# All expert weights of a fused attention and mixture-of-experts kernel pass through ten fixed staging places

## The chip, the cores and the metric

The kernel runs on 1 core of a Trainium2 chip. The metric is the device time of one execution in microseconds (us). The engines are TensorE (PE, matmuls; PEld is its weight load), VectorE (DVE), ScalarE (ACT), GpSimd (POOL) and SyncE (SP, which here only issues DMAs and register loads). Each engine works through its own list of instructions strictly in the order in which it is written, so an instruction that waits also holds whatever stands behind it.

## The reference, cut to what matters

```python
scores = scale * np.matmul(q, k.transpose(0, 1, 3, 2))       # 8 batches, 8 heads, 576 x 64
thresh = np.max(scores, axis=-1, keepdims=True) - tau
scores = np.where(scores >= thresh, scores, -1000000000.0)
attn = softmax(scores)
x = (attn @ v) as 4608 tokens x 512
logits = x @ w_gate ; expert_idx = argmax(logits)            # 8 experts, one for each token
for e in range(8):
    h = np.maximum(x[mask_e] @ w1[e], 0.0)                   # 512 -> 1024
    out[mask_e] = gate_w * (h @ w2[e])                       # 1024 -> 512
```

## The kernel before, in words

**Attention.** The 64 heads are taken in 32 pairs, n = 0 to 31, each in 11 steps (NSTEP), so the attention ends with step 352 (KEND). In a step PE forms a tile of scores of a later pair (s_unit, for the row maxima), a tile of transposed scores of the present pair (st_unit), and parts of the product with v (av_piece). Every operand is split into a high and a low 16-bit part. The operand tiles of four pairs rotate: QK (high and low parts of q and k), ck and CQ (low parts, constants and the rows of maxima), each refilled by DMAs on SP's queue (stack, parts). vf holds v of one group.

**Routing of a batch.** When the last head of a batch has left PSUM (evac), finish scales the tokens: row sums `rs` (L519, L520, L524, L525), tokens `xn` (L534), and their 16-bit parts into the rows `R` (L541 on ACT, L542 on DVE for the last batch). Each tile of 128 tokens is transposed by a DMA on SP's queue into `xTg` (L549); logits multiplies it by w_gate on PE (`lg`, L567, 12 small matmuls for each tile), route finds the expert on DVE (L597 to L608), and ranks counts on PE (`rk`, L616 to L619) where each token goes. send scatters the rows to a table in DRAM (L639), tables2 and tables3 work out which rows each block of an expert gathers, and fetch gathers them (L863) and transposes them (`xTm` or `spare`, L873).

**Experts.** Blocks of 128 tokens: four for each of experts 0 and 1, one at a time (g = 0 to 7), later ones in pairs. The first two blocks of expert 1 and all of expert 0 hold tokens that were placed before the last batch was routed, so their matmuls stand between the steps of that routing on PE. gemm1 makes `h` (L927, 96 matmuls of 128x128 for a block of 128), relu splits it into `hl` (L915 on ACT, L916 on DVE), gemm2 makes `y` (L960, 24 matmuls of 512 columns), leave scales it into `o` (L971).

**Weights.** An expert has 8 pieces of 512 KB (w = 0, 1 for w1 and w2, c = 0 to 3), listed in wseq. load_w reads a piece as 32-bit numbers into a staging tile, split_w makes its high part on ACT (L822) and its low part on DVE (L830; for expert 0 with a helping matmul, L256 and L257) into `wb1` or `wb2` of set e % 2. Expert 0's pieces pass through two tiles of the pool mp0 and, for its last two, through ck and CQ. The pool mp1, on the space that the attention's tiles leave (close), holds eight staging tiles for all later pieces; expert 1's eight loads are issued there from ACT's queue, everything later from SP's, each when the piece eight places earlier has been split (weights).

The order of each engine's list is set by a scheduler from the planned steps, so small moves in the plan can reorder instructions of all engines near the end of the attention.

Of the kernel before, what the change touches and what calls it, by code (L numbers as in the profile page):

```python
# [9 lines left out]
F16 = mybir.dt.float16  # L10
F32 = mybir.dt.float32
# [6 lines left out]
P = 128  # L18
B, H, S, D = 8, 8, 576, 64
DM, E, F = 512, 8, 1024  # L20
NTOK = B * S
NPAIR = B * H // 2
# [22 lines left out]
TUNE = dict(  # L45
    lead=10, cast=2, sl=8, ll=15, sp0=3, sps=0, lv=-16, sv0=-6, sv1=2, av=2, g=4, l=3, d=4, g5=4, l5=3, d5=2, g6=1, l6=2, d6=2, g7=1, l7=1, d7=1, off=2, off5=1, off6=5, lg=4, lg7=22, km=12, rate=40, dh=1, do=3, ws0=6, wsd=2, w1d=4, plv=1, xv=5, so=0, sto=0, ord=0, sc=6, fa=3, fd=4, wa1=-70, wa2=-86, wl1=-28, wl2=-6, avb=1, route=1, ranks=7, pp=8, ew=4, maskat=0, w1a=-38, w1b=4,
)
# [3 lines left out]
def kernel(  # L51
# [9 lines left out]
    nc = tc.nc  # L61
# [13 lines left out]
    apool = ExitStack()  # L75
    ldp = ExitStack()
    ld = ldp.enter_context(tc.tile_pool(name="ld", bufs=2, side="right"))
    xp = ctx.enter_context(tc.tile_pool(name="xp", bufs=2))
    op = apool.enter_context(tc.tile_pool(name="op", bufs=4))
    pp = apool.enter_context(tc.tile_pool(name="pp", bufs=8))  # L80


# [23 lines left out]
    NB = 2  # L106
    NQ = 4
    ck2 = [cpool.tile([P, 2, 2, S], F16, name=f"ck_{i}") for i in range(NQ // 2)]
    cq2 = [op.tile([P, 2, 9 * P], F16, tag=f"CQ{i}", name=f"CQ_{i}", bufs=1) for i in range(NQ // 2)]
    cks = [[ck2[i // 2][:, i % 2, a] for a in range(2)] for i in range(NQ)]  # L110
    cqs = [cq2[i // 2][:, i % 2] for i in range(NQ)]
    none = before[96:96 + NM, 0:64]
# [53 lines left out]
    gr = {}  # L166
# [10 lines left out]
    def plan(k, f, where=END):  # L177
        if urgent[0]:
            f = hurry(f)
        assert (k, where) >= (now[0], slot[0])  # L180
        acts.setdefault(k, ([], [], []))[where].append(f)
# [11 lines left out]
    def after(k, f, where=END):  # L193
        plan(now[0] + k, f, where)
# [27 lines left out]
        st[n] = dict(qkf=qkf, Ph={}, Pl={})  # L222

    def load_v(g):
        vf = op.tile([P, 2, 10, D], F32, tag="vf", name=f"vf_{g}", bufs=1)
        load = (nc.sync if g == 0 else nc.scalar).dma_start(vf, v[g])
        if g == 0:
            tc.keep_in_program_order(load)
        gr[g] = dict(vf=vf)

    def split(n, lag=1):

# [26 lines left out]
    def stack(n):  # L259
        d = st[n]  # L260
        hi, lo = d["hi"], d["lo"]
        d["CK"] = cks[n % NQ]
        d["QA"], d["KB"] = [], []

        d["CQ"] = CQ = cqs[n % NQ]
        if n >= NQ:
            nc.sync.dma_start(
                CQ[64:KC].rearrange("p (t c) -> p t c", t=18), none.unsqueeze(1).to_broadcast([NM, 18, 64])
            )
        for a in range(2):  # L270
            r = slice(64 * a, 64 * a + 64)
            QK = op.tile([P, 2, S], F16, tag=f"QK{a}", name=f"QK_{n}_{a}")
            nc.sync.dma_start(QK[0:64], hi[r])
            nc.sync.dma_start(QK[64:128, 0], lo[r, 0])
            nc.sync.dma_start(QK[64:128, 1], hi[r, 1])
            nc.sync.dma_start(d["CK"][a][0:64], lo[r, 1])
            d["QA"].append(QK[:, 0])
            d["KB"].append(QK[:, 1])
        for a in range(2):
            r = slice(64 * a, 64 * a + 64)  # L280
            nc.sync.dma_start(CQ[0:64, a * NT * P:(a + 1) * NT * P], hi[r, 0, 0:NT * P])
            nc.sync.dma_start(CQ[0:64, 8 * P + 64 * a:8 * P + 64 * a + 64], hi[r, 0, NT * P:S])

    def split_v(g, u):
        d = gr[g]
        vf = d["vf"]
        d["vop"] = vop = vops[g % NB]
        tc.keep_in_program_order(nc.scalar.activation(vop[:, u, :, 0:D], vf[:, u], AF.Copy, scale=SV))
        for i in range(2):
            t = slice(5 * i, 5 * i + 5)  # L290
            after(1, lambda i=i, t=t: low_part(
                vf[:, u, t], vop[:, u, t, 0:D], vop[:, u, t, D + 1:2 * D + 1], SV, f"v{g}_{u}_{i}"
            ), END if i else MID)
# [477 lines left out]
    NS = NEARLY + NL  # L771
    EARLY_SLOTS = sum(EARLY[1])
    wb1, wb2, pools = [], [], []
    slots = {}
    placed = {}

# [7 lines left out]
    wq = {}  # L784
    T = {}

    def open_pool(i):

        mp = ctx.enter_context(
            tc.tile_pool(name=f"mp{i}", bufs=2, side=("right", "left")[i], reuse_waits="tile")  # L790
        )
        pools.append(mp)
        wb1.append(mp.tile([P, 4, 2 * F], F16, name=f"wb1_{i}", bufs=1))
        wb2.append(mp.tile([P, 4, 2 * F], F16, name=f"wb2_{i}", bufs=1))

    def load_w(e, w, c):

        i = int(e != 0)
        if (e, w) == (0, 1) and c >= 2:
            wf = (ck2, cq2)[c - 2][0]  # L800
            wf = wf.rearrange("p a b s -> p (a b s)") if c == 2 else wf.rearrange("p a s -> p (a s)")
            wq[e, w, c] = wf = wf.bitcast(F32)[:, 0:F]
            nc.sync.dma_start(wf, w12[e, :, c, w])
            return
        wq[e, w, c] = wf = pools[i].tile([P, F], F32, tag="wf", name=f"wf_{e}_{c}_{w}", bufs=2 + 6 * i)
        if e in range(E):
            load = (nc.scalar if e == 1 else nc.sync).dma_start(wf, w12[e, :, c, w])
            if e == 1:
                tc.keep_in_program_order(load)
            return  # L810
        if e not in regs:
            regs[e] = nc.sync.value_load(T["esi"][0:1, e - E:e - E + 1], min_val=0, max_val=E - 1)
        nc.sync.dma_start(wf, w12[ds(regs[e], 1), :, c, w].rearrange("o p f -> (o p) f"))
# [185 lines left out]
    NSTEP = len(st_order)  # L999
# [4 lines left out]
    KEND = NSTEP * NPAIR  # L1004
    KM = KEND - TUNE["km"]
    NF = 3
    WS0, WSD = TUNE["ws0"], TUNE["wsd"]
    W1D = TUNE["w1d"]
    DH, DO = TUNE["dh"], TUNE["do"]
    PLV = {(NPAIR - 1, t) for t in ((), (1, REST), (1,), (REST,), (1, REST, 5), (1, 3, REST, 5, 7))[TUNE["plv"]]}  # L1010
    XV = {(B - 1, j) for j in range(TUNE["xv"])}
# [84 lines left out]
    def close():  # L1096
        apool.close()
        open_pool(1)
        for i, x in enumerate(wseq[8:16]):
            after(W1D * i, lambda x=x: load_w(*x))  # L1100

    wseq = [(0, w, c) for w in range(2) for c in range(4)]
    k = NSTEP * (NPAIR - 2) - LEAD - SL
    plan(k + 1, room)
    for i in range(8):
        t = k + WS0 + WSD * i if i < 4 else KEND + 1 + 2 * (i - 4)
        plan(t, lambda i=i: split_w(*wseq[i]))
        if i < 4:
            plan(t, lambda i=i: load_w(*wseq[i + 2]))
        elif i >= 6:  # L1110
            plan(NSTEP * (NPAIR - 2) + i - 4, lambda i=i: load_w(*wseq[i]))
    TABLES = {B - 3: tables0, B - 2: tables1, B - 1: tables2}
    plan(KEND + 12, close)

# [56 lines left out]
        last = -1 if e2 < 0 else NE * e2 + NE - 1 if e2 < E else NEARLY + e2 - E  # L1171
        return wseq[turn[0]] == (e, w, c) and (e, w, c) in wq and past[w] >= last

    asked = [8]

    def weights(j):
        turn[0] = j + 1
        split_done.add(wseq[j])
        split_w(*wseq[j])
        if j + 8 < len(wseq):  # L1180
            k, e = when[j][:2]
            moe(
                max(chunk[0] + 1, k - (14 if e == 2 else 24)) if e < E else chunk[0] + 1,
                lambda: asked[0] == j, lambda: (asked.__setitem__(0, j + 1), load_w(*wseq[j + 8])),
            )

    for j, (k, *x) in enumerate(when):
        moe(k, lambda x=x: may(*x), lambda j=j: weights(j + 8))

# [131 lines left out]
```

## Time and profile before

| what | value |
|---|---|
| time, median of 3 runs | 1016.65 us (1015.65 to 1017.06) |
| profiled execution, its own time | 1016.57 us |
| its span, first to last instruction | 1014.8 us |
| PE busy, share of the span | 949.3 us, 94% |
| DVE, ACT, POOL busy | 699.2, 653.9, 558.2 us |
| mean granted clock of PE, of full speed | 0.979 |

The profile divides the span into busy time of each engine; idle time in front of an instruction is put down to what it waited for last. The time of an execution holds 1.8 us around the span.

### The profile page before, as it was taken

The page shows a single profiled execution, that of the slowest core. Times are in us where ns is not written, and L with a number is a line of the kernel's source. Part 1 is how long each engine was busy: PE and PEld are TensorE (multiplying, and loading weights), DVE is VectorE, ACT ScalarE, POOL GpSimd, SP SyncE. Part 2 cuts the span into 40 slices and gives each one's busy share as a digit, 9 for nine tenths or more (in the row PEclk, how much of TensorE's full clock was granted, in tenths as well). Part 3 has the DMA queues.
Part 4 walks back from the last instruction along what each step waited for, and adds up shares of the span by engine and source line. Part 5 has one row for each costly group of instructions (what it writes and reads, how often), then busy time and mean ns, then how long its engine had stood idle before and what let it go on. Part 6 is the DMA issues. An engine that isn't in the chain of part 4 may idle for free. (4 is left out here: it accounts for less than half of the span.)

```text
span 1014.8 us, 28646 instructions
## 1 busy us (share of the span) xinstructions
PE 949.3 (94%) x11548; PEld 610.5 (60%) x11548; DVE 699.2 (69%) x1413; ACT 653.9 (64%) x1114; POOL 558.2 (55%) x470
## 2 busy tenths in 40 slices
PE   7799999999999999999998995979999999999997
PEld 2355555556565565565565863657766676667684
DVE  7899999988999898999996853715342433424560
ACT  2689897988988888989898843314342433424551
POOL 6466885996987969969879820341212222222121
PEclk9899999999999999999998998889999999999999
DMA  7553554563746645636458299788565755557730
GB/s 199 145 135 76 138 140 126 131 166 104 184 102 176 135 122 151 176 109 166 101 156 209 66 217 249 262 166 223 176 166 162 226 143 182 151 163 219 224 106 26
DMA packets 142749, 159.19 MB, mean 157 GB/s; under 512 B 96403, under 2 KB 112789, under 8 KB 142614
## 3 DMA queue, kind: packets, MB, share of 16 engines
q1 hardware_dynamic: 125446, 96.13, 38.2%
q10 hardware_dynamic: 7920, 31.74, 10.8%
q0 software_dynamic: 9248, 29.45, 8.9%
q8 instruction: 92, 1.51, 0.7%
q14 instruction: 43, 0.35, 0.1%
HBM read 90.24 MB, written 19.44 MB: 108 GB/s over the span
## 5 line engine op out<-in xcount | busy, mean ns | idle before, releaser
L436 POOL TENSOR_TENSOR pl<-e,ph 128x1024 f16<-128x1024 f32 x158 | 336.0, 2135 | 101.4 <-ACT ph L435 62.4
L427 ACT ACTIVATE e<-st,ntau 128x512 f32<-128x512 f32 (+1 forms) x352 | 222.8, 650 | 49.3 <-PE st L411 45.8
L430 DVE SCALAR_TENSOR_TENSOR e<-st,e 128x512 f32<-128x512 f32 (+1 forms) x352 | 219.8, 636 | 13.1 <-ACT e L427 12.5
L927 PEld LDWEIGHTS <-wb 128*128 128x128 f16 x2304 | 191.5, 99 | 31.5 <-issue 13.0
L927 PE MATMUL h<-xTm,wb 128*128 128x256 f16 (+2 forms) x2112 | 200.3, 254 | 8.7 <-issue 8.6
L960 PE MATMUL y<-wb,hl 128*128 128x512 f16 (+1 forms) x1056 | 205.2, 364 | 0.8 <-issue 0.8
L370 DVE TENSOR_REDUCE nm<-s 128x1 f32<-128x512 f32 x300 | 188.2, 633 | 19.1 <-PE s L360 17.0
L480 PE MATMUL av<-vop,ph 128*128 128x65 f16 (+3 forms) x3072 | 188.6, 195 | 3.0 <-ACT x L490 2.0
L480 PEld LDWEIGHTS <-ph 128*128 128x128 f16 (+1 forms) x3072 | 159.7, 100 | 48.3 <-issue 23.3
L480 PE MATMUL av<-vop,pl 128*128 128x65 f16 (+1 forms) x1536 | 168.3, 195 | 5.1 <-POOL pl L436 5.0
L435 ACT CAST ph<-e 128x1024 f16<-128x1024 f32 x160 | 166.4, 1040 | 6.6 <-DVE e L430 6.1
L480 PEld LDWEIGHTS <-pl 128*128 128x128 f16 (+1 forms) x1536 | 137.4, 100 | 36.4 <-issue 10.7
L960 PEld LDWEIGHTS <-hl 128*128 128x128 f16 (+1 forms) x1056 | 94.8, 101 | 101.2 <-issue 7.1
L830 DVE SCALAR_TENSOR_TENSOR wb<-wf,wb 128x1024 f16<-128x1024 f32 x88 | 104.0, 1221 | 68.2 <-ACT wb L822 65.6
L410 PE MATMUL st<-QK 128*128 128x512 f16 (+3 forms) x640 | 138.3, 293 | 3.3 <-DVE nm L370 0.9
L411 PE MATMUL st<-CQ,ck 128*128 128x512 f16 (+3 forms) x640 | 137.2, 288 | 2.3 <-issue 1.6
L974 POOL DMA_INDIRECT out_dram<-o,gt x40 | 43.4, 1085 | 167.5 <-ACT o L971 149.3
L358 PE MATMUL s<-QK 128*128 128x512 f16 (+1 forms) x600 | 129.1, 292 | 3.6 <-DVE e L430 2.7
L360 PE MATMUL s<-ck,CQ 128*128 128x512 f16 (+1 forms) x600 | 127.4, 287 | 1.5 <-DMA CQ<-hi 1.5
L915 ACT ACTIVATE hl<-h 128x512 f16<-128x512 f32 (+1 forms) x80 | 45.9, 573 | 120.5 <-PE h L927 97.9
L822 ACT ACTIVATE wb<-wf 128x1024 f16<-128x1024 f32 x94 | 95.9, 1051 | 37.1 <-DMA wf<-in_w_dram 19.3
L971 ACT ACTIVATE o<-y,gt 128x512 f32<-128x512 f32 (+1 forms) x40 | 26.6, 664 | 101.0 <-PE y L960 80.0
(199 smaller groups left out, 995.5 us busy)
## 6 DMA issues: line engine op xcount, KB each, us to landing
wf<-in_w_dram SPq DMA_DIRECT2D x86, 512.0 KB
qkf<-in_qk_dram ACTq DMA_DIRECT2D x30, 576.0 KB
vf<-in_v_dram ACTq DMA_DIRECT2D x15, 640.0 KB
QK<-hi SPq DMA_DIRECT2D x64, 144.0 KB
QK<-lo SPq DMA_DIRECT2D x64, 72.0 KB
QK<-hi SPq DMA_DIRECT2D x64, 72.0 KB
ck<-lo SPq DMA_DIRECT2D x64, 72.0 KB
CQ<-hi SPq DMA_DIRECT2D x64, 64.0 KB
```

Of the source, the lines that this page charges most:

```text
L358: nc.tensor.matmul(sc[rows, oc], d["QA"][a][:, cols], d["KB"][a][:, CH[c]], start=True, stop=False)
L360: nc.tensor.matmul(sc[rows, oc], d["CQ"][:, at:at + cols.stop - cols.start], d["CK"][a][:, CH[c]], start=False, stop=True,)
L370: nc.vector.tensor_reduce(o, sc[:, 0:width(t)], axis=AX.X, op=ALU.max, negate=True)
L410: nc.tensor.matmul(sc[rows, oc], d["KB"][a][:, cols], d["QA"][a][:, CH[c]], start=True, stop=False)
L411: nc.tensor.matmul(sc[rows, oc], d["CK"][a][:, cols], d["CQ"][:, q], start=False, stop=True)
L427: nc.scalar.activation(pf, sc, AF.Exp, bias=ntau, scale=0.125 / SS)
L430: nc.vector.scalar_tensor_tensor(pf, sc, 0.0, pf, ALU.is_ge, ALU.mult)
L435: nc.scalar.copy(h, pd)
L436: (nc.vector if (n, t) in PLV else nc.gpsimd).tensor_tensor(l, pd, h, ALU.subtract)
L480: nc.tensor.matmul(av[:, 0:D] if z == 2 else av, l if z == 1 else h, vop[:, tv, W:W + D] if z == 2 else vop[:, tv, 0:W], start=i in (0, NT ...
L927: nc.tensor.matmul(o, Wt[:, c, wh, f], x, start=c == 0 and z == 0, stop=c == 3 and z == 2,)
L960: nc.tensor.matmul(o, h[:, hh], Wt[:, f, wh, c], start=f == 0 and z == 0, stop=f == 7 and z == 2)
```

## The change

All weight pieces of all experts pass through ten fixed places (`stages`): the tiles of ck, CQ and QK of the attention, vf, and the two tiles of mp0. The attention's tiles become permanent (op moves to the outer pool, and QK is one tile of two halves for each of four pairs), and mp1 has no staging tiles any more. Expert 1's eight loads move from ACT's queue to SP's and are planned at steps 340 to 362 (the end of the attention is step 352); two pieces of expert 2 follow at once. A later piece j + 10 is asked for when piece j has been split, where it was j + 8. Expert 0's first splits move by up to four steps. Only load_w, the plan and the allocation change: what is multiplied and split stays the same.

```diff
-    op = apool.enter_context(tc.tile_pool(name="op", bufs=4))
+    op = ctx.enter_context(tc.tile_pool(name="op", bufs=1))
...
+    qks = [op.tile([P, 2, 2, S], F16, name=f"QK_{i}") for i in range(NQ)]
+    vf = op.tile([P, 2, 10, D], F32, name="vf")
...
+        if i == 0:
+            first_wf.extend(mp.tile([P, F], F32, name=f"wf_{z}", bufs=1) for z in range(2))
+            stages.extend([words(ck2[0], "a b s"), words(cq2[0], "a s"), words(qks[0], "a w s"), words(qks[1], "a w s")])
+            stages.append(vf.rearrange("p u t d -> p (u t d)")[:, 0:F])
+            stages.extend([words(qks[2], "a w s"), words(qks[3], "a w s"), words(cq2[1], "a s"), *first_wf])
...
-        wq[e, w, c] = wf = pools[i].tile([P, F], F32, tag="wf", name=f"wf_{e}_{c}_{w}", bufs=2 + 6 * i)
+        j = 6 + 4 * w + c if e == "x" else wseq.index((e, w, c))
+        wq[e, w, c] = wf = first_wf[j % 2] if j < 6 else stages[(j - 6) % len(stages)]
         if e in range(E):
-            load = (nc.scalar if e == 1 else nc.sync).dma_start(wf, w12[e, :, c, w])
+            load = nc.sync.dma_start(wf, w12[e, :, c, w])
...
         open_pool(1)
-        for i, x in enumerate(wseq[8:16]):
-            after(W1D * i, lambda x=x: load_w(*x))
...
-        t = k + WS0 + WSD * i if i < 4 else KEND + 1 + 2 * (i - 4)
+        t = k + (5, 7, 14, 16)[i] if i < 4 else KEND + 1 + 2 * (i - 4)
...
-            plan(t, lambda i=i: load_w(*wseq[i + 2]))
-        elif i >= 6:
-            plan(NSTEP * (NPAIR - 2) + i - 4, lambda i=i: load_w(*wseq[i]))
+            plan(t + 3, lambda i=i: load_w(*wseq[i + 2]))
+    for i, t in enumerate((336, 338, 340, 342, 344, 346, 356, 358, 360, 362)):
+        plan(t, lambda i=i: load_w(*wseq[6 + i]))
...
+    def ask(j):
+        if j < len(wseq):
+            k, e = when[j - 8][:2]
             moe(
-                max(chunk[0] + 1, k - (14 if e == 2 else 24)) if e < E else chunk[0] + 1,
-                lambda: asked[0] == j, lambda: (asked.__setitem__(0, j + 1), load_w(*wseq[j + 8])),
+                max(chunk[0] + 1, k - (16 if e == 2 else 24)) if e < E else chunk[0] + 1,
+                lambda: asked[0] == j, lambda: (asked.__setitem__(0, j + 1), load_w(*wseq[j])),
             )
```

**ACT, where the attention's last product has left PSUM.** Before, the row sums of the last batch (L519, L524) follow that evacuation at once, and ACT issues expert 1's first two loads (L807) itself:

```order
909 L490 COPY x_12084<-av_1_13212 128x4x65
910 L495 COPY xh_10427<-av_1_13212 64x65 x2
911 L519 ACTIVATE rs_13369<-x_12084 128x32
912 L524 ACTIVATE rs_13369<-xh_10427 128x8
913 L807 DMA wf_0_0_13393<-in_w_dram 128x1024
914 L915 ACTIVATE hl_0_13258<-h_1_13261 128x512
915 L541 CAST R<-xn_0_13410 128x4x128
916 L541 CAST R<-xn_1_13424 128x4x128
917 L807 DMA wf_1_0_13463<-in_w_dram 128x1024
918 L822 ACTIVATE wb_1_13390<-wf_0_0_13393 128x1024
```

The same place in the changed kernel, right after L490, L495 and two splits into wb_1 like the first row (its line 825 is line 822 of before, 918 is 915; vf, QK, CQ and wf are the staging places of expert 1's pieces):

```order
914 L825 ACTIVATE wb_1_13318<-vf 128x1024
915 L825 ACTIVATE wb_1_13318<-QK_121 128x1024
916 L825 ACTIVATE wb_1_13319<-QK_122 128x2x512
917 L519 ACTIVATE rs_13298<-x_11995 128x32
918 L825 ACTIVATE wb_1_13319<-CQ_118 128x2x512
919 L825 ACTIVATE wb_1_13319<-wf_11588 128x2x512
920 L524 ACTIVATE rs_13298<-xh_10360 128x8
921 L918 ACTIVATE hl_0_13186<-h_1_13189 128x512
922 L918 ACTIVATE hl_0_13392<-h_0_13323 128x512
923 L918 ACTIVATE hl_0_13392<-h_1_13395 128x512
924 L825 ACTIVATE wb_1_13319<-wf_11589 128x2x512
925 L541 CAST R<-xn_0_13336 128x4x128
```

Five of expert 1's splits now stand ahead of L519, two more ahead of L524, and the eighth, of wf_11589, ahead of the first cast of the rows (L541). On DVE the low parts of the same pieces stand in the same way ahead of L520, L525 and L542.

**SP, around the transposes of the last batch.** Before, the five transposes into xTg (L549) stand among those of gathered rows (spare, xTm), and the loads of experts 2 and 3 come behind them all:

```order
531 L873 DMA_TRANSPOSE spare<-spare 128x8x128
532 L549 DMA_TRANSPOSE xTg_0_13444<-R 128x8x128 x2
533 L873 DMA_TRANSPOSE spare<-spare 128x8x128
534 L873 DMA_TRANSPOSE xTm_13543<-Rm_13542 128x8x128
535 L549 DMA_TRANSPOSE xTg_2_13491<-R 128x8x128 x2
536 L549 DMA_TRANSPOSE xTg_4_13520<-R 128x8x128
537 L873 DMA_TRANSPOSE xTm_13774<-Rm_13773 128x8x128
538 L807 DMA wf_0_0_13674<-in_w_dram 128x1024
```

The same place in the changed kernel, right after the two spare transposes (line 810 is line 807 of before, 876 is 873):

```order
527 L810 DMA wf_11589<-in_w_dram 128x1024
528 L876 DMA_TRANSPOSE xTm_13465<-Rm_13464 128x8x128
529 L876 DMA_TRANSPOSE xTm_13685<-Rm_13684 128x8x128
530 L810 DMA QK_119<-in_w_dram 128x1024
531 L810 DMA QK_120<-in_w_dram 128x1024
532 L810 DMA vf<-in_w_dram 128x1024
533 L810 DMA QK_121<-in_w_dram 128x1024
534 L810 DMA QK_122<-in_w_dram 128x1024
535 L810 DMA CQ_118<-in_w_dram 128x1024
536 L810 DMA wf_11588<-in_w_dram 128x1024
537 L810 DMA wf_11589<-in_w_dram 128x1024
538 L549 DMA_TRANSPOSE xTg_0_13370<-R 128x8x128 x2
```

Expert 1's last piece (row 527) follows the two spare transposes, and eight loads of experts 2 and 3 (rows 530 to 537, each into a place that a split of expert 1 frees) now stand ahead of the five transposes into xTg.

On PE the same 72 matmuls `y` stand between the end of the attention and `rk` in both kernels, and 160 `h` before, 156 now; but 96 of the `h` and 62 of the `y` now come ahead of the first `lg`, where 60 and 48 did.

## Rows read from the trace of the kernel before

**Rows 1.** Stretches: length, busy us of each engine, granted clock, DMA share, GB/s.
```profile
584.00:594.00 10.00, 7.91 (x148) 6.90 (x145) 4.88 (x13) 4.58 (x11) 5.13 (x7) 1.00 0.76 204
...
625.00:635.00 10.00, 0.28 (x7) 0.11 (x4) 5.03 (x12) 5.20 (x7) 1.11 (x1) 0.74 1.01 394
635.00:640.00 5.00, 5.00 (x55) 4.33 (x56) 3.54 (x8) 1.83 (x3) 0.00 (x0) 0.50 1.01 406
...
645.00:655.00 10.00, 8.65 (x107) 6.31 (x105) 6.49 (x28) 3.15 (x7) 5.02 (x5) 1.00 0.93 354
...
660.00:684.00 24.00, 18.32 (x172) 12.22 (x170) 3.69 (x15) 2.48 (x4) 11.21 (x17) 0.87 0.86 176
...
725.00:750.00 25.00, 25.00 (x182) 17.55 (x180) 8.07 (x12) 9.16 (x12) 6.82 (x9) 1.00 0.45 115
```

**Rows 2.** Timeline of PE: start us, us, instructions, [idle before, releaser].
```profile
594.48 10.52 PE L960 MATMUL y<-wb,hl 128*128 128x512 f16 x48
...
604.84 3.51 PE L927 MATMUL h<-spare,wb 128*128 128x128 f16 x60
...
616.27 0.48 PE L567 MATMUL lg<-wg,xTg 128*128 128x8 f16 x12 [2.92 <-DMA xTg<-R]
...
634.95 0.19 PE L616 MATMUL rk<-oh,before 128*128 128x8 f16 x1 [9.72 <-DVE lg L604]
...
635.51 3.57 PE L927 MATMUL h<-spare,wb 128*128 128x128 f16 x32
...
644.68 0.28 PE L927 MATMUL h<-xTm,wb 128*128 128x128 f16 x2
...
689.03 10.64 PE L927 MATMUL h<-xTm,wb 128*128 128x256 f16 x96
```

**Rows 3.** Timeline of DVE, same columns.
```profile
599.53 0.68 DVE L542 TENSOR_TENSOR R<-xn,R 128x512 f16<-128x512 f32 x1
...
629.77 2.36 DVE L830 SCALAR_TENSOR_TENSOR wb<-wf,wb 128x1024 f16<-128x1024 f32 x2 [6.55 <-ACT wb L822]
632.05 0.19 DVE L597 TENSOR_REDUCE mx<-lg 128x5 f32<-128x40 f32 x1
...
634.46 0.23 DVE L604 TENSOR_REDUCE lg<-oh 128x8 f32<-128x40 f16 x1
```

**Rows 4.** Timeline of ACT and of its DMA issues (ACTq), same columns.
```profile
586.80 0.26 ACT L519 ACTIVATE rs<-x 128x32 f32<-128x32 f32 x1
...
612.05 0.33 ACTq L807 DMA_DIRECT2D wf<-in_w_dram  x1
...
620.91 1.06 ACT L822 ACTIVATE wb<-wf 128x1024 f16<-128x1024 f32 x1 [5.36 <-DMA wf<-in_w_dram]
628.68 2.95 ACT L822 ACTIVATE wb<-wf 128x1024 f16<-128x1024 f32 x3 [6.72 <-DMA wf<-in_w_dram]
```

**Rows 5.** Tile wf, 585 to 632 us: durations (ns, least/median/most), then who waited.
```profile
L822 ACT ACTIVATE wb<-wf x10: 1041/1056/1057, 592.0 to 630.6; 128x1024 f16<-128x1024 f32 x10
L830 DVE SCALAR_TENSOR_TENSOR wb<-wf,wb x9: 1215/1225/1226, 594.2 to 630.9; 128x1024 f16<-128x1024 f32 x9
...
  DVE wb L830: 22.3, 5
  ACT wb L822: 17.8, 5
```

**Rows 6.** Timeline of SP's DMA issues, same columns (a long issue is one that waits).
```profile
554.09 12.55 SPq L873 DMA_TRANSPOSE xTm<-Rm  x3
588.04 1.23 SPq L873 DMA_TRANSPOSE spare<-spare  x1
592.43 4.26 SPq L549 DMA_TRANSPOSE xTg<-R  x2
...
599.49 12.06 SPq L549 DMA_TRANSPOSE xTg<-R  x3
...
616.30 31.87 SPq L807 DMA_DIRECT2D wf<-in_w_dram  x16
```

More of the change, by code (lines that the diff above doesn't have):

```diff
@@ L108 @@
     ck2 = [cpool.tile([P, 2, 2, S], F16, name=f"ck_{i}") for i in range(NQ // 2)]
-    cq2 = [op.tile([P, 2, 9 * P], F16, tag=f"CQ{i}", name=f"CQ_{i}", bufs=1) for i in range(NQ // 2)]
+    cq2 = [op.tile([P, 2, 9 * P], F16, name=f"CQ_{i}") for i in range(NQ // 2)]
+    qks = [op.tile([P, 2, 2, S], F16, name=f"QK_{i}") for i in range(NQ)]
+    vf = op.tile([P, 2, 10, D], F32, name="vf")
     cks = [[ck2[i // 2][:, i % 2, a] for a in range(2)] for i in range(NQ)]
@@ L224, in load_v @@
     def load_v(g):
-        vf = op.tile([P, 2, 10, D], F32, tag="vf", name=f"vf_{g}", bufs=1)
         load = (nc.sync if g == 0 else nc.scalar).dma_start(vf, v[g])
@@ L228, in load_v @@
             tc.keep_in_program_order(load)
-        gr[g] = dict(vf=vf)
+        gr[g] = {}
     def split(n, lag=1):
@@ L271, in stack @@
             r = slice(64 * a, 64 * a + 64)
-            QK = op.tile([P, 2, S], F16, tag=f"QK{a}", name=f"QK_{n}_{a}")
+            QK = qks[n % NQ][:, a]
             nc.sync.dma_start(QK[0:64], hi[r])
@@ L285, in split_v @@
         d = gr[g]
-        vf = d["vf"]
         d["vop"] = vop = vops[g % NB]
@@ L773, with words @@
     wb1, wb2, pools = [], [], []
+    first_wf, stages = [], []
+    def words(x, dims):
+        return x.rearrange(f"p {dims} -> p ({dims})").bitcast(F32)[:, 0:F]
     slots = {}
@@ L794, in open_pool @@
         wb2.append(mp.tile([P, 4, 2 * F], F16, name=f"wb2_{i}", bufs=1))
-    def load_w(e, w, c):
[L798 to L804, printed above, removed]
-        wq[e, w, c] = wf = pools[i].tile([P, F], F32, tag="wf", name=f"wf_{e}_{c}_{w}", bufs=2 + 6 * i)
+        if i == 0:
[3 more added lines that the diff above has]
+            stages.extend([words(qks[2], "a w s"), words(qks[3], "a w s"), words(cq2[1], "a s"), *first_wf])
+    def load_w(e, w, c):
+        j = 6 + 4 * w + c if e == "x" else wseq.index((e, w, c))
+        wq[e, w, c] = wf = first_wf[j % 2] if j < 6 else stages[(j - 6) % len(stages)]
         if e in range(E):
-            load = (nc.scalar if e == 1 else nc.sync).dma_start(wf, w12[e, :, c, w])
+            load = nc.sync.dma_start(wf, w12[e, :, c, w])
             if e == 1:
@@ L1172, in may @@
         return wseq[turn[0]] == (e, w, c) and (e, w, c) in wq and past[w] >= last
-    asked = [8]
+    asked = [16]
     def weights(j):
@@ L1179, in weights @@
         split_w(*wseq[j])
-        if j + 8 < len(wseq):
-            k, e = when[j][:2]
-            moe(
-                max(chunk[0] + 1, k - (14 if e == 2 else 24)) if e < E else chunk[0] + 1,
-                lambda: asked[0] == j, lambda: (asked.__setitem__(0, j + 1), load_w(*wseq[j + 8])),
-            )
+        ask(j + len(stages))
+    def ask(j):
+        if j < len(wseq):
+            k, e = when[j - 8][:2]
+            moe(
+                max(chunk[0] + 1, k - (16 if e == 2 else 24)) if e < E else chunk[0] + 1,
+                lambda: asked[0] == j, lambda: (asked.__setitem__(0, j + 1), load_w(*wseq[j])),
+            )
+    for j in range(2):
+        ask(16 + j)
     for j, (k, *x) in enumerate(when):
```

2 lines of the change are left out of this document (removed).

## The prediction

> **What bounds the kernel now.** I read the stretches first. From 725 us on PE is busy 25.00 us of 25.00 [rows 1]: there the matmuls are the time, and a change of staging can win nothing. Between the end of the attention and 689 us they are not. PE is busy 7.91 us of the ten from 584, 0.28 of the ten from 625, 8.65 of the ten from 645 and 18.32 of the 24 from 660, and from 635 to 640 it has a granted clock of 0.50, the lower of its two levels (1.2 GHz), after those ten idle microseconds [rows 1]. So the question is what held PE there. PE's timeline names two waits: 2.92 us for a transpose into xTg, and 9.72 us in front of `rk`, for DVE's L604 [rows 2]. DVE's timeline shows why L604 came so late: the routing's first step, L597, starts at 632.05, right behind two low parts of expert 1's weights (L830), for which DVE had waited 6.55 us, and L604 starts at 634.46 [rows 3]. The last `lg` had been there since about 619.5 (the fourth starts at 616.27, and one tile and six `y` follow [rows 2]); the routing waited not for its data but in DVE's list behind weights. ACT's timeline goes one step further back: it waited 5.36 and 6.72 us for wf; the eighth load was issued at 612.05 and used at 628.68 [rows 4]. In all ACT waited 17.8 us for these pieces and DVE 22.3 us for ACT [rows 5]. Expert 1's weights are late, and the routing of the last batch pays for it.
>
> **What the change does to this.** Six of expert 1's pieces go into places that are free before the attention ends, a seventh into one that the first split of expert 0's w2 frees; only the eighth is issued after 588 us, behind the spare transposes (the first at 588.04 [rows 6]). Seven splits can thus run as soon as the last product is out, at 586.80 where L519 stood [rows 4], and DVE's list has no late weight ahead of L597. Expert 2's first splits there must wait for the end of `h` of block 3, which the walk below puts at 610, ahead of the `lg`.
>
> *PE's walk to rk.* I price the matmuls by their starts: 48 `y` from 594.48 to 604.84 are 0.216 us each; 60 `h` in 3.51 us are at most 0.0585; a tile's 12 `lg` at most 0.48 [rows 2]. The list from 594.48 to `rk` is 72 `y`, 156 `h`, 5 `lg` tiles: 15.6 + 9.1 + 2.4 = 27.1, so `rk` could start at 621.6 instead of 634.95. The 62 `y` and 96 `h` ahead of the first `lg` bring PE there at 594.48 + 13.4 + 5.6 = 613.5; the fifth is wanted at 613.5 + 4 x 0.48 + 10 x 0.216 = 617.6.
>
> *Are the transposes there by then?* Before, rows were ready from L519 at 586.80 to the last L542 at 599.53 + 0.68 = 600.2 [rows 3, 4]. Now five splits of 1.056 us delay L519 by 5.3 us, and DVE's seven of 1.225 us end at 586.8 + 1.06 + 8.6 = 596.4 [rows 4, 5], where DVE's first token tile follows; three relus and the eighth split come between. Counting DVE's list from there (15 instructions, the plain ones by L542's 0.68) the last row is ready near 607, 7 us later than before. The eight loads ahead of the transposes on SP can go from about 595 on, the last when the eighth split is done, near 601. At 394 GB/s, which the stretch from 625 moved [rows 1], 512 KB take 1.33 us, eight of them 10.6, so they end near 606. A transpose takes 1.23 us at least (the issue [rows 6]). At most it is what five `xTg` and two others took from 592.43 until the fifth `lg` at about 619.1, 26.7 us [rows 2, 6], less seven loads of 1.33 beside them: 17.4 / 7 = 2.5. Five end between 613 and 619.5: a wait on PE of 0 to 2 us; I take 1.
>
> *Other gaps on the way.* From 584 to 594 PE lost 2.1 us in a run of `h` while the DMA engines became busy [rows 1]. The run before `lg` is now longer (90 `h` nearly in a row), so I take 1 us of this, 0 to 3. `rk` then starts at 621.6 + 2 = 623.6: **-11.4 us**, bounds -13.4 and -4 (the latter with the slow transposes of the rival below).
>
> *The clock behind rk.* Without ten idle microseconds the matmuls after `rk` run at the full clock. From 635.51 to 644.68 PE took 9.17 us for 32 `h` and 24 `y` [rows 2], which are 1.9 + 5.2 = 7.1 by the prices above: **-2.1 us** (0 if PE idles as long elsewhere).
>
> *From there to 689.03.* 44.35 us [rows 2] for 288 `h` and 72 `y`, which are 32.4 by the same prices: 12 us are lost. Part is while loads and scattered rows keep the DMA engines at 0.93 (645 to 655), more while the gathers and transposes of the next blocks run (660 to 684, share 0.86 [rows 1]). The second cause stays. Of the first, eight of the sixteen loads that SP issued from 616.30 in 31.87 us [rows 6] are gone from there. I take **-1.5 us**, between -6 and +2.
>
> *The end of the attention* is a bound from both sides: the lists are the same up to about 525 us, then expert 0's splits move and more 512 KB loads share SP's queue with the transposes into xTm, which SP issued from 554.09 [rows 6]; one of them now stands behind a place that the last but one pair must leave. PE could wait up to 3 us for it, or gain 1; I take **+0.8 us**.
>
> *Behind 689 us* I take nothing: PE is full, so ten places for eight hide behind matmuls. If that cover failed, a late load would cost its 1.33 us each.
>
> Sum: -11.4 - 2.1 - 1.5 + 0.8 = -14.2. The profiled execution took 1016.57 us, 0.08 less than the median of 1016.65, so I subtract from it: **1002.4 us**.
>
> **The rivals.** *Late transposes.* Expert 1's loads came from another queue than the transposes, beside them; now eight loads stand ahead of the transposes in one queue. Before, 19 us passed between the last row (600.2) and the fifth `lg` at about 619.1 [rows 2, 3]. If that holds again from 607 on, the fifth is there at 626; `rk` follows 60 `h` later with part of them at the lower clock, at about 632, a gain of 3. The other terms give -2.1 - 1.5 + 0.8, so about 1011 us. Against it: most of expert 1's loads and another transpose shared those 19 us, and none need do so now. The Trainium skill speaks for this rival, in "DMA: Bandwidth & Descriptors", section "Queues, rings and completion order": an engine takes turns between queues, but within one queue's ring it takes descriptors in order, so loads of another queue only share with a transpose while loads of its own go first. That long transposes and loads overlapped in this trace agrees with it; no row shows one queue alone. The same page (section "Latency and other measured facts") gives 261 GB/s for a transpose, by which 256 KB would take 1.0 us, an estimate; by that the sum would be 1001.
>
> *Slower: the eighth piece.* ACT's list has its split ahead of the first cast of rows, so the whole routing waits for this one load, queued on SP behind the spare transposes. I expect it issued near 590.6 and landed near 596. Before, the eighth took 628.68 - 612.05 = 16.6 us from issue to use [rows 4]. That again would be 607; the rows would be ready at 618, the fifth transpose 19 us later, `rk` at 642 and the time near 1023 us, with the idle clock back. It decides from a landing near 603 (slow transposes) to 608 on. Against it: those 16.6 us were shared with SP's loads from 616.30 [rows 6], which now come behind it.
>
> *Nothing gained.* If the gap in front of `rk` were refilled by something else in the list (tables of the routing, another wait of ACT), the time would stay near 1016; nothing in the rows asks for it.
>
> *More gained.* If the loads move out of the way of the `h` runs as well, 6 of the 12 us behind `rk` come back and no transpose waits: 997 us.
>
> **How the numbers follow.** My forecast 0.57 (998 to 1007), late transposes 0.18, more gained 0.15, slower 0.06, nothing gained 0.04. The range 995 to 1011 leaves out the last two and the far half of the late transposes. About 0.2% (2 us) can be told from no change: faster 0.90, the same 0.04, slower 0.06.
>
> **What would show it.** Right: ACT's seven splits directly behind the last evacuation with no wait for a load; L597 on DVE without L830 that waited ahead of it; `rk` between 621 and 627 with at most 1 us of wait for DVE; the clock at 1.00 behind it; 725 us and later unchanged. Wrong: PE waiting over 5 us at `lg` for xTg (late transposes); ACT waiting over 5 us at the eighth split (slower); a wait of PE before 580 us over 3 us.

## The result, and the profile after

The changed kernel takes 1004.85 us (median of 7 runs, 1003.13 to 1012.18) against 1016.04 us for the kernel before, measured with it (7 runs): a ratio of 0.990, 95% interval 0.987 to 0.993. Run again later, with its variants, it took 1006.74 us against 1013.44 us, a ratio of 0.994 (0.991 to 0.996). The profiled execution took 1003.13 us, the shortest of the seven; its span is 1001.3 us, 13.5 us less than before. Of two variants below, one execution each was far slower than the others (1825.04 and 1024.01 us), and it is left out of their medians and ratios.

I read the windows first, the same ones as [rows 1] (here of PE alone: length, busy us, granted clock, DMA share, GB/s):

```profile
584.00:594.00 10.00, 8.78 (x183) 1.00 0.74 223
625.00:635.00 10.00, 10.00 (x146) 0.95 0.50 194
635.00:640.00 5.00, 5.00 (x50) 1.00 0.72 184
645.00:655.00 10.00, 7.79 (x72) 1.00 0.79 189
660.00:684.00 24.00, 24.00 (x222) 1.00 0.83 217
725.00:750.00 25.00, 25.00 (x165) 1.00 0.68 195
```

The hole from 625 to 635 is filled, the clock behind it is 1.00, and 660 to 684, where before 18.32 of 24 us were busy at a clock of 0.87, is full. PE's timeline of the changed kernel shows the same points as [rows 2] (`h` is now L930, `y` L963):

```profile
562.93 0.83 PE L930 MATMUL h<-xTm,wb 128*128 128x128 f16 x12 [2.70 <-DMA xTm<-Rm]
...
587.63 3.52 PE L930 MATMUL h<-xTm,wb 128*128 128x128 f16 x60
...
618.44 0.46 PE L567 MATMUL lg<-wg,xTg 128*128 128x8 f16 x12 [3.33 <-DMA xTg<-R]
...
623.13 3.73 PE L963 MATMUL y<-wb,hl 128*128 128x512 f16 x10
...
630.35 0.17 PE L616 MATMUL rk<-oh,before 128*128 128x8 f16 x1
...
654.01 0.22 PE L930 MATMUL h<-xTm,wb 128*128 128x128 f16 x1 [1.51 <-issue]
...
675.57 10.64 PE L930 MATMUL h<-xTm,wb 128*128 128x256 f16 x96
```

The first row past the attention starts at 587.63, where it started at 584.71 before. `rk` starts at 630.35 and waits for nothing. But PE now waits at `lg`: 6.3 us in four waits for xTg, and the ten `y` behind them take 3.73 us, 0.373 each where [rows 2] gives 0.216. From `rk` to the first `h` of 256 columns it is 45.22 us, where it was 54.08. Behind that row nothing changed: 325.7 us to the end of the span, 325.8 before.

The lists of ACT and of DVE (start, us, instruction, [idle before, releaser]) show whether the weights still hold the routing:

```profile
593.34 0.24 ACT L519 ACTIVATE rs<-x 128x32 f32<-128x32 f32 x1
593.49 1.04 ACT L825 ACTIVATE wb<-CQ 128x1024 f16<-128x1024 f32 x1
594.44 1.04 ACT L825 ACTIVATE wb<-wf 128x1024 f16<-128x1024 f32 x1
...
600.33 1.06 ACT L825 ACTIVATE wb<-wf 128x1024 f16<-128x1024 f32 x1 [3.15 <-DMA wf<-in_w_dram]
```

```profile
608.60 0.69 DVE L542 TENSOR_TENSOR R<-xn,R 128x512 f16<-128x512 f32 x1 [0.72 <-ACT R L541]
...
618.41 1.23 DVE L833 SCALAR_TENSOR_TENSOR wb<-QK,wb 128x1024 f16<-128x1024 f32 x1
...
627.24 0.20 DVE L597 TENSOR_REDUCE mx<-lg 128x5 f32<-128x40 f32 x1 [7.00 <-PE lg L567]
628.66 0.24 DVE L604 TENSOR_REDUCE lg<-oh 128x8 f32<-128x40 f16 x1
```

They don't. In [rows 3] L597 stood right behind a late weight; now the last weight ahead of it (L833, of expert 2) is done at 619.6, and L597 waits 7.00 us for PE. ACT's one wait for a piece is 3.15 us, at the eighth. What is late now shows on SP's queue:

```profile
594.71 0.57 SPq L810 DMA_DIRECT2D wf<-in_w_dram  x1
595.38 4.75 SPq L876 DMA_TRANSPOSE xTm<-Rm  x2
...
603.60 0.86 SPq L810 DMA_DIRECT2D wf<-in_w_dram  x2
604.56 16.87 SPq L549 DMA_TRANSPOSE xTg<-R  x5
```

The last row was ready at 609.3 (L542 above), but the five transposes were issued until 621.4. One by one:

```profile
604.56 5.18 SPq L549 DMA_TRANSPOSE xTg<-R  x1
609.83 5.08 SPq L549 DMA_TRANSPOSE xTg<-R  x1
615.00 2.48 SPq L549 DMA_TRANSPOSE xTg<-R  x1
617.57 2.51 SPq L549 DMA_TRANSPOSE xTg<-R  x1
620.17 1.26 SPq L549 DMA_TRANSPOSE xTg<-R  x1
```

One transpose alone takes 1.23 us [rows 6]. Each of these has its row of tokens by the time its issue begins, and each issue begins 0.1 us behind the end of the one before, so the time is not a wait for a semaphore, as the caption of [rows 6] would have it: it is within the issues. Ahead of them in SP's queue stand eight loads (six of expert 2 and two of expert 3), issued from 600.23 to 604.5. By their completion marks in the trace the last of these landed at 615.1, and the transposes at 618.4, 620.6, 621.2, 622.8 and 623.5; the four `lg` that wait start right behind the first four. What holds an issue for 5 us, no row shows. The windows (as above) show the DMA engines moving 404 and 345 GB/s until 613, and then 142:

```profile
604.00:609.00 5.00, 5.00 (x57) 1.00 1.01 404
609.00:613.00 4.00, 4.00 (x61) 1.00 1.06 345
613.00:617.00 4.00, 2.11 (x10) 1.00 1.25 142
```

### The profile page after: what moved, and what is told of

Its sections match the earlier page's. It is cut to its first block, busy times and chain, and to the rows that moved or that the text cites. A ratio compares the mean times of both kernels' runs of the same rounds, so it can differ in the third digit from the quotient of the medians.

```text
span 1001.3 us, 28641 instructions
## 1 busy us (share of the span) xinstructions
PE 941.8 (94%) x11548; PEld 606.9 (61%) x11548; DVE 699.8 (70%) x1413; ACT 652.8 (65%) x1114; POOL 560.6 (56%) x470
## 3 DMA queue, kind: packets, MB, share of 16 engines
q1 hardware_dynamic: 126598, 100.33, 40.2%
## 5 line engine op out<-in xcount | busy, mean ns | idle before, releaser
L430 DVE SCALAR_TENSOR_TENSOR e<-st,e 128x512 f32<-128x512 f32 (+1 forms) x352 | 219.5, 635 | 11.4 <-ACT e L427 11.0
L930 PEld LDWEIGHTS <-wb 128*128 128x128 f16 x2304 | 189.7, 98 | 28.0 <-issue 9.4
L930 PE MATMUL h<-xTm,wb 128*128 128x256 f16 (+2 forms) x2112 | 198.0, 254 | 7.2 <-issue 4.5
L963 PE MATMUL y<-wb,hl 128*128 128x512 f16 (+1 forms) x1056 | 203.2, 362 | 0.0
L963 PEld LDWEIGHTS <-hl 128*128 128x128 f16 (+1 forms) x1056 | 94.6, 100 | 99.4 <-issue 4.2
L919 DVE SCALAR_TENSOR_TENSOR hl<-h,hl 128x512 f16<-128x512 f32 (+1 forms) x80 | 52.3, 660 | 61.1 <-ACT hl L918 60.8
L358 PEld LDWEIGHTS <-QK 128*128 128x128 f16 x600 | 46.0, 99 | 43.6 <-issue 25.1
```

The source lines that it names most:

```text
L358: nc.tensor.matmul(sc[rows, oc], d["QA"][a][:, cols], d["KB"][a][:, CH[c]], start=True, stop=False)
L430: nc.vector.scalar_tensor_tensor(pf, sc, 0.0, pf, ALU.is_ge, ALU.mult)
L930: nc.tensor.matmul(o, Wt[:, c, wh, f], x, start=c == 0 and z == 0, stop=c == 3 and z == 2,)
L963: nc.tensor.matmul(o, h[:, hh], Wt[:, f, wh, c], start=f == 0 and z == 0, stop=f == 7 and z == 2)
```

## The experiments

My theory was the prediction's: expert 1's weights are late, the routing pays for it, and loading them early cures it. The rival is that something that came along with it, the shared queue or the ten places, is the gain. The first four runs set early and late loads against the two queues; the others ask what holds the changed kernel now. Places in the trace are starts in PE's timeline of the profiled execution: the first `h` past the attention, `rk`, and the first `h` of 256 columns ("wide h"), from which all of them take 325.7 to 326.0 us to the end of the span. Each ratio is to runs of the kernel before that were taken together with that variant.

| kernel | median us | ratio to before (95%) | attention ends | rk | wide h |
|---|---|---|---|---|---|
| before | 1016.04 | 1 | 584.71 | 634.95 | 689.03 |
| changed | 1004.85 | 0.990 (0.987 to 0.993) | 587.63 | 630.35 | 675.57 |
| changed, again | 1006.74 | 0.994 (0.991 to 0.996) | 588.19 | 630.44 | 677.16 |
| late loads, SP's queue, ten places | 1005.50 | 0.989 (0.985 to 0.993) | 588.05 | 628.47 | 678.44 |
| before, with SP's queue alone | 1003.76 | 0.986 (0.982 to 0.990) | 587.74 | 628.81 | 678.52 |
| late loads, ACT's queue, ten places | 1012.47 | 0.996 (0.993 to 0.998) | 585.11 | 638.93 | 684.15 |
| early loads, ACT's queue, ten places | 1002.40 | 0.988 (0.985 to 0.991) | 587.91 | 629.53 | 675.87 |
| eight loads behind the transposes | 1002.43 | 0.985 (0.980 to 0.989) | 592.37 | 627.60 | 674.42 |
| first xTm ahead of two loads | 995.99 | 0.980 (0.977 to 0.984) | 590.69 | 625.07 | 666.53 |
| expert 0's old steps | 999.19 | 0.982 (0.979 to 0.986) | 587.35 | 629.42 | 671.32 |
| the last two together | 999.12 | 0.984 (0.982 to 0.987) | 589.60 | 630.63 | 672.85 |
| first xTm and last xTg ahead of loads | 1001.74 | 0.987 (0.984 to 0.990) | 593.84 | 627.05 | 674.36 |

**The early start undone.** The changed kernel, with expert 1's loads planned late as before:

```diff
     def close():
         apool.close()
         open_pool(1)
+        for i, x in enumerate(wseq[8:16]):
+            after(4 * i, lambda x=x: load_w(*x))
...
-    for i, t in enumerate((336, 338, 340, 342, 344, 346, 356, 358, 360, 362)):
+    for i, t in enumerate((336, 338)):
```

> The changed kernel with one part undone: expert 1's eight loads are planned at the end of the attention again, as before; the ten places and SP's queue stay. My theory (the gain is the late weights, gone from the lists of ACT and DVE): the splits wait again, rk falls back to 633 to 637 us behind a wait for DVE of over 7 us, the half clock behind rk is back, and the time is 1013 to 1019. Rival (the places, the queue or the earlier loads of expert 2 are the gain): rk stays near 630 and the time within 1003 to 1007.

1005.5 us: my theory missed, and the rival's number came. Yet the wait that it was about is there. DVE's timeline:

```profile
614.86 1.23 DVE L833 SCALAR_TENSOR_TENSOR wb<-vf,wb 128x1024 f16<-128x1024 f32 x1 [5.56 <-ACT wb L825]
...
623.44 1.22 DVE L833 SCALAR_TENSOR_TENSOR wb<-wf,wb 128x1024 f16<-128x1024 f32 x1
624.57 0.20 DVE L597 TENSOR_REDUCE mx<-lg 128x5 f32<-128x40 f32 x1
```

All of expert 1's weights stand ahead of L597 again, and L597 starts right behind the last one. But that one is through 7.5 us earlier than before: the last piece, issued at 612.51, landed 7.4 us later, and ACT splits it at 621.48. Before, the eighth piece took 13.4 us from its issue at 612.05 to its landing at 625.46, by its completion marks. And the transposes, now ahead of most loads, go out in 3.78 + 5.28 us, and PE waits for none of them past 590. So the routing starts no later than with early loads (624.57 against 627.24), and 3.82 us of wait for DVE are left in front of `rk`, where [rows 2] has 9.72. The run undoes only expert 1's part: expert 2's first two pieces are still issued early (584.96 and 587.22).

**The queue alone.** The kernel before, with one word changed:

```diff
-            load = (nc.scalar if e == 1 else nc.sync).dma_start(wf, w12[e, :, c, w])
+            load = nc.sync.dma_start(wf, w12[e, :, c, w])
```

> The kernel before with one edit: expert 1's eight loads are issued by SP's queue instead of ACT's; eight places, late loads and all splits where they were. Theory Q (the gain is the queue: in one queue expert 1's last pieces come ahead of expert 2's loads, where before two queues shared the engines): the eighth piece lands under 11 us after its issue (16.6 before), L597 starts by 625, rk by 630, and the time is 1003 to 1008. Theory P (the gain is the ten places): the pieces stay late, L597 at 629 to 633, and the time is 1013 to 1018.

Theory Q: 1003.76 us, L597 at 624.29, `rk` at 628.81, with 5.08 us of wait for DVE left there. With eight places and late loads this gives a gain as large as the whole change. SP's timeline:

```profile
602.51 4.86 SPq L549 DMA_TRANSPOSE xTg<-R  x3
607.47 4.12 SPq L807 DMA_DIRECT2D wf<-in_w_dram  x7
611.70 6.99 SPq L873 DMA_TRANSPOSE xTm<-Rm  x1
618.81 23.85 SPq L807 DMA_DIRECT2D wf<-in_w_dram  x15
```

The seven are the last six of expert 1 and the first of expert 2; the other loads follow from 618.81. By completion marks expert 1's eighth piece landed 10.1 us after its issue, at 620.69, and expert 2's first at 622.04; L597 stands behind both. Before, they landed at 625.46 and 628.66. The last three transposes take 4.86 us of issue here and 12.06 before [rows 6]: beside the loads of ACT's queue transposes were slow as well.

Those slow transposes also held ACT. In the kernel before, ACT issued its seventh load only at 611.56, and what followed had stood still:

```profile
612.00 0.69 ACT L971 ACTIVATE o<-y,gt 128x512 f32<-128x512 f32 x1 [4.69 <-DMA xTg<-R]
```

In the program that load waits for the DMA eight places ahead of it, on either queue, and this is a transpose that SP issued at 599.49 and that landed at 611.54.

**The places alone.** Late loads on ACT's queue again, ten places kept:

```diff
-            load = nc.sync.dma_start(wf, w12[e, :, c, w])
+            load = (nc.scalar if e == 1 else nc.sync).dma_start(wf, w12[e, :, c, w])
```

(on top of the late plan above).

> The changed kernel with expert 1's loads planned late as before and issued by ACT's queue as before; the ten places for all pieces stay, and with them the earlier loads of expert 2. Theory Q (the queue is the gain): the last piece ahead of L597 is late again, rk starts at 633 or later, and the time is 1012 to 1018. Theory P (the places are): rk by 630, and the time is 1003 to 1008.

Theory Q again: 1012.47 us, `rk` at 638.93. Two rows of PE, the second as of before with a wait for DVE:

```profile
624.52 0.48 PE L567 MATMUL lg<-wg,xTg 128*128 128x8 f16 x12 [12.54 <-DMA xTg<-R]
...
638.93 0.18 PE L616 MATMUL rk<-oh,before 128*128 128x8 f16 x1 [2.98 <-DVE run L608]
```

With two queues both things are late, the transposes (SP needed 12.63 us for two of them from 607.16) and the weights. And the weights are late above all because ACT stands still in front of its load into CQ (issued at 626.74): the DMA eight places ahead of that is a transpose that SP issued at 615.79 and that landed at 626.66.

```profile
627.15 0.60 ACT L918 ACTIVATE hl<-h 128x512 f16<-128x512 f32 x1 [7.88 <-DMA xTg<-R]
```

What is left, 0.4%, comes from behind `rk`: 45.22 us to the wide `h`, as in the changed kernel, where late loads on SP's queue need 49.97 with ten places and 49.71 with eight. So on SP's queue ten places don't shorten this stretch, and what makes it 45.22 us in this kernel no run shows.

**Early loads on the other queue.** The changed kernel with the same line as above, and nothing else.

> The changed kernel with expert 1's eight loads issued by ACT's queue again, at the same early steps; ten places. With this, late and early loads stand on either queue: late on ACT's queue with ten places took 1012.5 us, late on SP's 1005.5, early on SP's 1004.9. Theory 1 (early loads and the shared queue are two cures of one wait, each enough): the weights are there, L597 has no waiting split ahead, the transposes have eight loads fewer ahead of them on SP, and the time is 1000 to 1006. Theory 2 (only the queue matters): 1009 to 1015, as with late loads on ACT's queue.

Theory 1: 1002.4 us, L597 with no waiting weight ahead of it (it waits 7.64 us for PE's `lg`), as in the changed kernel. So early loads and the shared queue are two cures of one wait. Either is enough, and together they give no more than one: 0.988 (early loads alone), 0.989 and 0.986 (the queue alone, with ten and with eight places), 0.990 and 0.994 together.

**The eight loads behind the last transposes.** They are expert 2's last six and expert 3's first two.

```diff
+            with tc.issue_after(T["turned"]) if 18 <= j < 26 else ExitStack():
+                load = nc.sync.dma_start(wf, w12[e, :, c, w])
...
-                lambda: asked[0] == j, lambda: (
+                lambda: asked[0] == j and (not 18 <= j < 26 or "turned" in T), lambda: (
```

(`turned` is the last transpose into xTg.)

> The changed kernel with the eight loads of expert 2 (from its third piece on) that stand in SP's queue ahead of the last batch's transposes put behind them; all else as in the changed kernel. Theory A (these loads make the transposes late): PE's waits at lg for xTg, 6.25 us in all, fall to under 2.5, rk starts 3 to 5 us earlier (625 to 627) and the time is 1000 to 1003. Theory B (they are the reason why the stretch behind rk lost its gaps): rk is earlier too, but from rk to the first 256-wide h, 44.7 us now, gets 3 to 6 us longer, and the time is 1003 to 1007. Theory C (the rows are late, or the transposes have a pace of their own): the waits at lg stay above 5 us, and the time is that of the changed kernel within 1 us.

Theory A's part on the waits is right. The transposes go out as fast as they can, and PE waits for none of them past 590:

```profile
600.28 4.71 SPq L879 DMA_TRANSPOSE xTm<-Rm  x2
608.98 6.82 SPq L549 DMA_TRANSPOSE xTg<-R  x5
615.85 2.24 SPq L813 DMA_DIRECT2D QK<-in_w_dram  x2
```

6.82 us for five, where it was 16.87: the loads ahead had set their pace, not the rows or the transposes themselves. `rk` is 2.75 us earlier, although this kernel's attention ends 4.7 us later (PE waits 3.8 us for the first xTm). From `rk` to the wide `h` it is 46.82 us, 1.6 more than in the changed kernel but about as much as in its repetition (46.72), so theory B's price is not shown by this run. The time, 1002.43 us, lies in A's range, but `rk` gained less than A's 3 to 5 us.

**The first transposes ahead of two loads.** The changed kernel, with the wait of 2.70 us at 562.93 aimed at:

```diff
-            load = nc.sync.dma_start(wf, w12[e, :, c, w])
+            with tc.issue_after(T["row", 1]) if 10 <= j < 12 else ExitStack():
+                load = nc.sync.dma_start(wf, w12[e, :, c, w])
```

(`T["row", 1]` is the transpose of the second block of rows.)

> The changed kernel with the fifth and sixth load of expert 1 put behind the first two transposes into xTm in SP's queue. Theory (the end of the attention is 2.9 us later because loads stand ahead of these transposes): PE's wait of 2.70 us at 562.93 is under 0.5, the attention ends at 584.7 to 586 instead of 587.63, and the time is 1002 to 1004. Rival (the 2.9 us come from the splits of expert 0, which were planned at other steps, or are made up at the lg wait): the wait goes, and the time stays within 1 us of the changed kernel's.

The wait went, and the time is 8.9 us less than the changed kernel's, the lowest of all; but neither theory's reason holds. The attention doesn't end earlier, it ends at 590.69. The gain lies behind it, in both later stretches (length, PE busy, granted clock, DMA share, GB/s; the first of this kernel, the second of the changed one):

```profile
625.07:666.53 41.46, 40.45 (x462) 1.00 0.87 203
```

```profile
630.35:675.57 45.22, 41.90 (x444) 0.96 0.81 190
```

From the end of the attention to `rk` it is 34.38 us instead of 42.72. The moved loads let the scheduler write other lists: two `lg` tiles now stand between `h`, one wait of 1.24 us for xTg is left, and the fifth `lg` no longer has ten slow `y` ahead of it:

```profile
616.05 0.46 PE L567 MATMUL lg<-wg,xTg 128*128 128x8 f16 x12 [1.24 <-DMA xTg<-R]
...
620.43 0.45 PE L567 MATMUL lg<-wg,xTg 128*128 128x8 f16 x12
...
625.07 0.17 PE L616 MATMUL rk<-oh,before 128*128 128x8 f16 x1
```

Its repetition:

> The kernel with the first two transposes into xTm ahead of the fifth and sixth load of expert 1, once more: it was the fastest alone (ratio 0.980 to before), and with expert 0's steps of before added, which alone won 5.7 us, it came out slower (0.984). If its lead is of the order that it leaves in the lists: a ratio of 0.977 to 0.984 again. If its six executions happened to be fast ones: 0.984 to 0.990, that of the other variants.

998.97 us, ratio 0.985 (0.980 to 0.989), with the attention's end at 590.79 and the wide `h` at 667.16, as in the first. The places are steady. The ratio lies just inside the range of the second expectation, 0.984 to 0.990, but its interval covers most of the first as well; so part of this variant's lead in the table may be luck of its six executions.

**Expert 0's steps of before.**

```diff
-        t = k + (5, 7, 14, 16)[i] if i < 4 else KEND + 1 + 2 * (i - 4)
+        t = k + 6 + 2 * i if i < 4 else KEND + 1 + 2 * (i - 4)
```

> The changed kernel with the first four splits of expert 0 back at the steps of before, two apart. If their new steps delay the end of the attention (PE waits 2.8 us for ACT's split in front of hi_w, none of it before): that wait falls under 0.8 us, the attention ends 1.5 to 2.5 us earlier and the time is 1002 to 1004. If the loads in SP's queue delay it: the wait goes and the end of the attention stays at 587 to 589, the time at 1004 to 1006.

999.19 us, better than either theory. The wait for ACT's split fell to 0.8 us, but another (3.1 us for DVE's `e`) took its place, and the attention ends only 0.3 us earlier. The gain is behind `rk`: 41.90 us to the wide `h`.

**Both.** The last two edits together:

> The changed kernel with the two edits that gained most alone: expert 0's first splits at the steps of before (999.2 us) and the first two transposes into xTm ahead of the fifth and sixth load of expert 1 (996.0 us). If they remove different waits at the end of the attention: 990 to 995. If both only shift the same stretch: 995 to 1000. If the gain of either was the order of transposes and loads that it happened to leave behind, anything up to 1003.

999.12 us, no better than either alone. `rk` is at 630.63 and it is 42.22 us from there to the wide `h`: both only shift the same stretch.

**Both orders of SP's queue.** The first xTm ahead of two loads, and the last xTg ahead of eight:

> The changed kernel with both orders of SP's queue altered: the first two transposes into xTm ahead of the fifth and sixth load of expert 1, and the last batch's transposes ahead of eight loads of expert 2. If the two gains add (8.9 us and 1.8 us against the changed kernel when alone): 992 to 996. If the gain of the first came because its transposes at lg were earlier too (its waits there fell from 6.3 to 1.2 us), the second has nothing left to win: 995 to 998. If the eight loads, moved behind, stretch the matmuls behind rk: 997 to 1003.

1001.74 us: worse than the first edit alone. The two don't add: the attention ends at 593.84, and from `rk` it is 47.31 us again, with 4.2 us of gaps in `h`.

**The eighth piece earlier.** The last four loads of expert 1 planned a few steps earlier:

```diff
-    for i, t in enumerate((336, 338, 340, 342, 344, 346, 356, 358, 360, 362)):
+    for i, t in enumerate((336, 338, 340, 342, 344, 346, 354, 355, 356, 357)):
```

> The changed kernel with the last four loads of expert 1 planned a few steps earlier, so that the eighth piece stands ahead of the spare transposes in SP's queue. All theories expect ACT's 3.15 us of wait at the eighth split gone. If the rows set the pace of the last transposes (theory C), rows and transposes come 3 us earlier, the waits at lg fall to 3 to 4 us and the time is 1001 to 1003. If the loads of expert 2 ahead of them do (theory A), those loads move with the eighth split's place too, by 3 us at most, and the waits at lg fall by 1 to 3. If neither, nothing changes: 1004 to 1006.

This one tells nothing of the question. At these steps a low part of expert 0's w2 is formed after expert 1's piece has been loaded over its place. So it is made of the wrong weights, and this kernel no longer computes the same. It also waits for that load (2.87 us on DVE at 590.44) and holds the attention's end to 590.46. The eighth split has no wait, as expected, but L519 ahead of it is 4.1 us later; 1005.11 us.

**The changed kernel once more.**

> The changed kernel once more, on the same chip as its variants: 1003 to 1007 by its seven times so far. If its lead over them comes from the chip that they ran on, it moves with them.

1006.74 us; against the runs of before beside it, it is 6.7 us faster, where it was 11.2. Early loads on ACT's queue and the last two edits together ran beside it and keep their lead of 4.3 and 7.6 us.

## Why the prediction came out, and where its steps failed

1002.4 us were forecast and 1004.85 measured; the sum was -14.2 us, and the profiled spans differ by -13.5. That closeness is partly luck, in two ways. By the medians the gain is 11.2 us, and 6.7 when run again, so the profiled execution is a fortunate one. And the sum holds only because its terms were off in opposite directions: up to `rk` -10.6 us were forecast (-11.4 and +0.8) and -4.6 came, behind it -3.6 and -8.9 came.

**The chain** (late weights ahead of L597, 9.72 us at `rk`, the idle clock behind) was right in kind: the seven splits stand behind the last evacuation without a wait for a load, no waiting weight is ahead of L597, and `rk` waits for nothing; 725 us and later are full. `rk` missed its mark of 621 to 627 by 3 us. But the chain names the wrong piece. The split at 628.68 [rows 4], for which ACT had waited 6.72 us, is not of expert 1's eighth piece: it is of expert 2's first, wf_0_0_13674, the load that SP issued at 616.30 [rows 6] and that landed at 628.66. It stands in ACT's list between the splits of expert 1's seventh and eighth pieces, and the views, which leave the numbers of tiles out, show them alike. Expert 1's eighth had landed at 625.46, 13.4 us after its issue and not 16.6. So the two L830 that hold L597 [rows 3] are one of each expert, and the last 3.2 us of the wait are expert 2's. The change cures that too, since it loads expert 2's first two pieces at 584.67 and 587.08, but the prediction did not know it.

**`rk` 11.4 us earlier: 4.6.** Three sizes failed. The wait for transposes was taken as 1 us and is 6.3. The ten `y` behind it ran at the half clock (granted 0.50 from 620 to 625, behind six microseconds of which 1.57 were busy): 3.73 us instead of 2.16. And the attention ends 2.9 us later, which is in these 4.6. The rival *late transposes* had the right mechanism, with over 5 us at `lg` as its sign; its own numbers, the fifth transpose at 626 and `rk` at 632, were nearly met (the fourth `lg` that waits starts at 622.79, `rk` at 630.35). The estimate of 2.5 us for a transpose was not at fault: without loads ahead five take 6.82 us, 1.4 each. What failed is "they end near 606": the loads were issued later than forecast, from 600.23 to 604.5 behind two transposes into xTm, and landed until 615.1, and the transposes behind them took up to 5.18 us of issue each. The Trainium skill ("DMA: Bandwidth & Descriptors", section "Queues, rings and completion order") was cited for that rival: in one queue, what is ahead goes first. The run with the loads behind agrees: 6.82 against 16.87 us. Loads of the other queue slow transposes too, though: before, three took 12.06 us of issue [rows 6].

**The end of the attention +0.8: +2.9**, at the edge of its bound of 3: 2.70 us for xTm and, earlier, 2.4 for ACT's split. Two runs that took one of these waits away did not bring the end back, since other waits of PE took their place.

**Behind `rk` -2.1 - 1.5: -8.9.** This is where the missing time was. From `rk` to the wide `h` the windows give 54.08 us, 47.05 busy at a clock of 0.89 before, and 45.22 us, 41.90 busy at 0.96 after: 3.7 us less idle and 5.2 less busy, of which the clock accounts for some 3.5 (47.05 x 0.89 = 41.9 and 41.90 x 0.96 = 40.2 differ by only 1.7). I priced the clock only up to 644.68. The row of 660 to 684 in [rows 1] had a clock of 0.87 too, and I read only its busy time. That the chain is what shortened this stretch is not shown: late loads on ACT's queue with ten places, a run with neither cure, has the same 45.22 us, and late loads on SP's queue need 49.97 and 49.71.

**The cause** that the prediction gave for its number, the early start, is not needed. One word in the kernel before (the queue) gives the same time; so does the early start without the queue. What both have in common, by their timelines, is that the pieces that stand ahead of L597 are there sooner: by 622.04 with the queue alone, against 628.66 before, and so early with the change that L597 waits for PE instead. That the queue alone makes them faster because they now go ahead of the loads that used to travel beside them is argued from these landing times; no run isolates it. I had charged the shared queue only as a risk. The queue alone wins by another road than the change, though: 6.1 us at `rk` and 4.4 behind it, where the change has 4.6 and 8.9.

**Open:** why the variants with two transposes moved, or with expert 0's old steps, win another 5 to 9 us. Their stretch from `rk` to the wide `h` is 41.5 to 42.2 us with a clock of 1.00, that of the others 45 to 50 at 0.90 to 0.96. What shortened it from 54.08 to 45.22 in the changed kernel, the larger part of its gain, is open in the same way. Each edit changed the written order on several engines, and no run took a single list apart.

## What to carry to other kernels

When a wait is traced to late loads, find out first which ones: rows that leave out the numbers of tiles can hide that two experts' pieces stand in one list. Then ask what travels beside them: putting the urgent loads into the queue of those that compete, ahead of them, may be worth as much as new buffers and an earlier start. Before giving a transfer a place in a queue, look at what comes behind it there: here transposes with their data ready went out slowly behind bulk loads that nobody needed yet. A load can also hold the engine that issues it: ACT stood still for 4.69 and 7.88 us in front of loads that, in the program, waited for a slow transpose eight DMAs ahead. And price idle time together with the clock behind it, in every stretch whose row shows one below 1.00.

## What was unexpected of the hardware

Runs of 128-column `h` break up with nothing to wait for: matmuls come in groups of 1 to 6, some 0.75 us apart, as from 591.36 to 593.58 in the changed kernel (starts 591.36, 592.12, 592.85, 593.58; the idle time is put down to "issue"). Between 560 and 690 us these gaps take 8.6 us before, 4.5 in the changed kernel and 2.0 in the fastest variant. The same 96 `h` take 5.52 us when unbroken (665.03 in the changed kernel). They come while loads, gathers or transposes use the DMA engines, but not always then, and the 512-column `y` hardly show them (one gap of 0.8 us). What PE waits for there no row names, and no run took it apart.
